# Two row halves of the array for the rows of an attention chunk, one sum of logits per routing group, one reciprocal for three chunks

## The chip, the cores and the metric

The kernel runs on one core of one Trainium2 chip. The metric is the device time of one execution in microseconds; a time given for a kernel is the median of several. One further execution is recorded by the hardware profiler, and all rows below are from that one.

## The reference

Sliding-window attention over 8 batches, 8 heads, 576 positions and 64 columns per head, and behind it a mixture of 8 experts in which each token goes to one expert:

```python
scores = scale * np.matmul(q, k.transpose(0, 1, 3, 2))
bias = slopes[:, None, None] * (-np.abs(rel).astype(np.float32))[None, :, :]
mask = (rel >= 0) & (rel < window)                      # window = 128
scores = np.where(mask, scores + bias[None], -1000000000.0)
attn = np.exp(scores - np.max(scores, axis=-1, keepdims=True))
attn = attn / (np.sum(attn, axis=-1, keepdims=True) + 1e-09)
x = attn @ v                                            # to 4608 tokens of 8 * 64 = 512
...
logits = x @ w_gate                                     # 512 x 8
expert_idx = np.argmax(logits, axis=1)
gate_w = softmax(logits)[np.arange(N), expert_idx]
out[mask] = gate_w[mask, None] * (np.maximum(x[mask] @ w1[e], 0.0) @ w2[e])   # for each expert e
```

Everything is float32.

## The kernel before

The 4608 queries are cut into 36 chunks of 128. A chunk takes four blocks of 32 queries, all of one batch, except for four chunks (the tails) that hold 64 queries of each of two batches. For a chunk, the steps are these; `g` is one of two groups of four heads:

- `scores` (L167, L176) writes bias and q.k into PSUM, each of the four 64x64 quadrants of TensorE's array for itself. `weigh` folds the window (L189), takes the maximum (L192) and lets ScalarE write the exponentials `pe` and, as a by-product, their sums `rsum` (L198).
- `guard` (L182) adds 1e-9 to the eight sums of a chunk on GpSimd.
- `transposes` (L211) turns `pe` with full 128x128 matmuls; ScalarE copies the result to `pT` (L213), GpSimd cuts the two key blocks out of it (L221, L223).
- `av` (L239) multiplies with v. The result is x transposed and not yet divided by the sums: for pair `p` of heads, 64 partitions hold one head and 64 the other. ScalarE copies it to `xT` (L286).
- `rows` (L244 to L257) turns it back to one row per token. The reciprocal of the chunk's sums is taken (L246). For each pair `p` of heads one matmul (L249) multiplies `xT[:, p, :]` with `iw_sb[:, p, :]`, which holds a 128x128 identity and beside it the 16 columns of the gate weights of both heads of the pair, so that the 144 columns of output are the row and each head's part of the logits. VectorE multiplies the logits' part and then the rows with the reciprocals (L254).
- `done` sums the parts of the logits over the eight heads (L1220) and stores the row to DRAM (`xd`) from the SP queue. A row has four pieces of 129 numbers, the last number of the last piece being kept for the gate.

After the last chunk of a routing group (`GROUPS`: 5, 5, 5, 6, 6, 3, 5 and 1 chunks), `route` works out each token's expert and place. Its matmuls use spare columns of the bank that `rows` wrote (`spare`).

The order of all this is written out by hand. A chunk `ch` begins at step `4 * ch`; the table `LAGS` says how many steps later each part is issued (`rows` 17 steps later), and `SPLIT` names the chunks whose second exponentials are issued three steps in, with the copy of an older chunk between them. Each engine works its own queue in order.

Behind attention, the experts' two layers (L711, L907) run from gathered rows with weights that were split into two parts; this and the tables of `route` are not touched.

Of the kernel before, what the change touches and what calls it, by code (L numbers as in the profile page):

```python
# [21 lines left out]
QB = 32  # L22
NP = H // 2
XW = 128 + 2 * E
SUB = 129
PITCH = 4 * SUB

# [7 lines left out]

def attention(ctx, tc, st, qT, kT, v, iw, load_c2, chunk_done, chunks, begun):
    nc = tc.nc
# [73 lines left out]
    make_bias()  # L111
    eps_sb = const.tile([128, H], F32, name="eps_sb")
    nc.gpsimd.memset(eps_sb, 1.0e-9)
# [66 lines left out]

    def guard(rsum):
        nc.gpsimd.tensor_tensor(out=rsum, in0=rsum, in1=eps_sb, op=ALU.add)  # L182

    def weigh(g, pe, rsum, s_ps, m, tail, lo, hi, later=False, add=True):
        s4 = s_ps.rearrange("p c n x -> p (c n) x")
        if m > 0:
            w = hi - 128
            sh = [128, 4, w]
            nc.vector.copy_predicated(out=s4[:, :, 0:w], mask=(tail_sb if tail else fold_sb)[:, 0:w].unsqueeze(1).to_broadcast(sh),  # L189
                                      data=s4[:, :, 128:128 + w])  # L190
        nmax = small.tile([128, 4], F32, name="nmax")
        nc.vector.tensor_reduce(out=nmax, in_=s4[:, :, lo:lo + 128], axis=AX.X, op=ALU.max, negate=True)  # L192

        def exps(pairs=range(2)):
            for n in pairs:
                for c in range(2):
                    h = 4 * g + 2 * n + c
                    nc.scalar.activation(  # L198
                        out=pe[:, h, :], in_=s_ps[:, c, n, lo:lo + 128], func=AF.Exp,
                        bias=nmax[:, 2 * c + n:2 * c + n + 1], scale=1.0, **(dict(accum_out=rsum[:, h:h + 1]) if add else {}),  # L200
                    )
            if add and g and 1 in pairs:
                guard(rsum)

        return exps if later else exps()
# [20 lines left out]
    def av(subs, pT, x_ps, pairs):  # L226
# [5 lines left out]
        for p, b, q, kb in whole:  # L232
# [4 lines left out]
            for c in range(2):  # L237
# [4 lines left out]
                )  # L242

    def rows(ch, subs, xT, rsum):  # L244
        rinv = small.tile([128, H], F32, name="rinv")
        nc.vector.reciprocal(out=rinv, in_=rsum)  # L246
        st["r_ps"] = r_ps = ps_r.tile([128, NP, 256], F32, name="r_ps")
        for p in range(NP):
            nc.tensor.matmul(out=r_ps[:, p, 0:XW], lhsT=xT[:, p, :], rhs=iw_sb[:, p, :], start=True, stop=True)  # L249
# [38 lines left out]
    def do(k, ch):  # L288
        if k == 9:
            return copy_x(ch)  # L290
        if k > 10:
            h = slice(4 * k - 44, 4 * k - 40)
            nc.vector.tensor_reduce(out=sums[ch][:, h], in_=pes[ch][:, h, :], axis=AX.X, op=ALU.add)
            return guard(sums[ch]) if k == 12 else None
        if k == 10:
# [5 lines left out]
        if k in (0, 4):  # L301
            if k == 0:
                pes[ch] = pp.tile([128, H, 128], F32, name="pe")
                sums[ch] = small.tile([128, H], F32, name="rsum", bufs=8)
            live[ch] = scores(subs, k // 4)
# [5 lines left out]
        elif k == 3:  # L311
            rows(ch, subs, xTs.pop(ch), sums.pop(ch))
        elif k == 6:
            transposes(subs, 1, pes[ch] if ch in SUMS else pes.pop(ch), pTs[ch])
        elif k == 7:
            xps[ch] = bank() if ch else ps_r.tile([128, NP, 256], F32, name="r_ps")[:, :, 0:128]
# [141 lines left out]
def spare(st, k, n):  # L458
    if st["step"] >= FREE_T:
        return st["bank"]()[:, k, 0:n]  # L460
    return st["r_ps"][:, k, XW:XW + n]

# [731 lines left out]
def attn_moe_kernel(ctx, tc, qT, kT, v, c2, iw, w12, out):  # L1194
# [9 lines left out]
    with ExitStack() as actx:  # L1204
        lgp = actx.enter_context(tc.tile_pool(name="lg", bufs=2))

        def begun(k):
            if k == 0:
                moe_setup(ctx, tc, st)
            else:  # L1210
                for j, n in enumerate(("tokh", "tokl")):
                    keep(tc, nc.vector.tensor_copy(out=st["hl"][:, :, j], in_=st[n]))

        def done(ch, subs, x_sb):
            c0, G = next((c, n) for c, n in GROUPS if c <= ch < c + n)
            g = ch - c0
            if g == 0:
                lgs["lg"] = lgp.tile([128, G, E], F32, name="lg")
            lg = lgs["lg"]
            nc.vector.tensor_reduce(out=lg[:, g, :], in_=x_sb[:, :, 128:XW].rearrange("q p (c e) -> q e p c", c=2),  # L1220
                                    axis=AX.XY, op=ALU.add)
            for lo in (0, 2):
                if lo == 2 and subs[0][0] == subs[2][0]:
# [3 lines left out]
                nc.sync.dma_start(out=st["xd"][t0:t0 + n].rearrange("t (p x) -> t p x", p=NP),  # L1227
                                  in_=x_sb[QB * lo:QB * lo + n, :, 0:SUB])
            if g == G - 1:
                groups = []  # L1230
# [16 lines left out]

        attention(actx, tc, st, qT, kT, v, iw, load_c2, done, chunks, begun)
    st["rc"] = ctx.enter_context(tc.tile_pool(name="rc", bufs=1))
# [6 lines left out]
def consts(moe_w_gate, moe_w1, moe_w2):  # L1256
# [4 lines left out]
    wg = moe_w_gate.reshape(NP, 128, E).transpose(1, 0, 2)  # L1261
    gate = np.zeros((128, NP, 2, E), wg.dtype)
    for c in range(2):
        gate[64 * c:64 * c + 64, :, c] = wg[64 * c:64 * c + 64]
    iw = np.concatenate([np.broadcast_to(np.eye(128, dtype=wg.dtype)[:, None], (128, NP, 128)), gate.reshape(128, NP, 2 * E)], axis=-1)
    parts = dict(ident=np.eye(128), seq=np.broadcast_to(np.arange(MAXOV), (128, MAXOV)), prof=np.broadcast_to(CAPS, (128, E)), rev=np.broadcast_to(np.arange(E, 0, -1), (128, E)), tokh=-64 * (back // 64), tokl=-(back % 64),
# [27 lines left out]
```

## Time and profile before

| | us |
|---|---|
| median of 3 runs (647.05 to 647.61) | 647.56 |
| profiled execution | 646.91 |
| its span, first to last instruction | 645.2 |
| TensorE busy in the span | 632.1 |
| VectorE busy | 390.9 |
| ScalarE busy | 314.1 |
| GpSimd busy | 299.2 |
| L249, 288 instructions, sum of their lengths | 41.4 |

In the rows, PE is a matmul on TensorE, PEld a load of its weights, which runs beside the matmuls. A form such as `64*128 128x72` is the rows and columns of the array that are used, and the output. One f32 matmul of the program shows as two loads and two matmuls. Lengths of matmuls overlap, since the array is a pipeline: the pace is read from the distance between starts. In grouped rows, "| a, b | c" is busy us in all, mean ns of one, and idle us of the engine just ahead, with what ended that.

### The profile page before, as it was taken

How to read it: one execution, taken by the hardware profiler on the slowest of the kernel's cores; microseconds unless marked ns; L12 is line 12 of the kernel's file. 1: busy time of each engine (PE TensorE's matmuls, PEld its weight loads, DVE VectorE, ACT ScalarE, POOL GpSimd, SP SyncE). 2: the span in 40 equal slices, each digit the busy share in tenths (PEclk: the TensorE clock that was granted, in tenths of full speed). 3: DMA queues.
4: the chain of work that ended last, by engine and by line, in shares of the span. 5: the costliest groups of instructions: out<-in, count | busy, mean ns of one | idle time of the engine just before them, and what ended most of it. 6: DMA issues, size and time to landing. Idle time of an engine off the chain costs nothing.

```text
span 645.2 us, 15063 instructions
## 1 busy us (share of the span) xinstructions
PE 632.1 (98%) x5681; PEld 540.2 (84%) x5681; DVE 390.9 (61%) x978; ACT 314.1 (49%) x947; POOL 299.2 (46%) x414
## 2 busy tenths in 40 slices
PE   8999999999998999999999999999999999999995
PEld 4888888888887988888988898898898888888884
DVE  6578888969898785545544654555455355346411
ACT  5878889888867324433333334334233333424311
POOL 5534657769446040166236707633660660561202
PEclk9999999999999999999999999999999999999999
DMA  9958998988734263372534325333442542534101
GB/s 312 301 153 216 220 260 237 217 258 240 193 69 103 54 196 98 130 273 75 186 128 151 108 78 183 113 94 139 142 122 83 165 122 87 185 107 143 65 0 62
DMA packets 57645, 97.90 MB, mean 152 GB/s; under 512 B 11669, under 2 KB 31765, under 8 KB 56674
## 3 DMA queue, kind: packets, MB, share of 16 engines
q1 hardware_dynamic: 49090, 76.89, 39.9%
q0 software_dynamic: 8336, 19.76, 10.6%
q8 instruction: 46, 0.75, 0.5%
q10 hardware_dynamic: 144, 0.26, 0.2%
q14 instruction: 29, 0.24, 0.1%
HBM read 77.91 MB, written 18.98 MB: 150 GB/s over the span
## 4 chain that ended last, share of the span: by engine, by line
PE 67%; ACT 0%; DVE 0%; issue 0%; POOLq 0%; POOL 0%; ACTq 0%
PE y_ps L907 32%; PE l_ps L711 30%; PE s_ps L711 2%; PE x_ps L672 1%; PE b_ps L239 1%; PE y_ps L867 1%; PE r_ps L249 0%; PE x_ps L867 0%; ACT pe L198 0%; POOLq L1060 0%; PE l_ps L683 0%; DVE y L915 0%; DVE nmax L192 0%; ACT e_xh L674 0%; DVE s_ps L189 0%
## 5 line engine op out<-in xcount | busy, mean ns | idle before, releaser
L714 ACT ACTIVATE hh<-l_ps 128x336 fp32r<-128x336 f32 (+7 forms) x104 | 45.9, 446 | 203.4 <-PE l_ps L711 176.9
L718 DVE SCALAR_TENSOR_TENSOR hl<-l_ps,hh 128x336 fp32r<-128x336 f32 (+7 forms) x104 | 51.7, 501 | 152.4 <-ACT hh L714 137.5
L691 POOL DMA_INDIRECT xg<-xd,od_idx x112 | 114.8, 1025 | 35.1 <-issue 34.8
L198 ACT ACTIVATE pe<-s_ps,nmax 128x128 f32<-128x128 f32 x288 | 102.9, 382 | 33.7 <-DVE nmax L192 27.0
L907 PE MATMUL y_ps<-wh,hh 128*128 128x512 f32 (+5 forms) x280 | 111.0, 397 | 0.0
L907 PE MATMUL y_ps<-wh,hl 128*128 128x512 f32 (+5 forms) x280 | 110.4, 394 | 0.0
L907 PE MATMUL y_ps<-wl,hh 128*128 128x512 f32 (+5 forms) x280 | 110.3, 394 | 0.0
L895 POOL DMA_INDIRECT out<-y,od_pidx x33 | 34.6, 1049 | 147.8 <-ACT y L913 141.2
L999 DVE TENSOR_TENSOR wl<-w_raw,wh 128x512 fp32r<-128x512 f32 x114 | 73.9, 690 | 32.0 <-ACT wh L995 27.4
L711 PE MATMUL l_ps<-xh,wh 128*128 128x304 f32 (+9 forms) x416 | 81.8, 318 | 0.3 <-DVE hl L718 0.3
L711 PE MATMUL l_ps<-xl,wh 128*128 128x304 f32 (+9 forms) x416 | 81.1, 316 | 0.3 <-issue 0.3
L711 PE MATMUL l_ps<-xh,wl 128*128 128x304 f32 (+9 forms) x416 | 81.0, 317 | 0.0
L711 PEld LDWEIGHTS l_ps<-xh,wh 128*128 128x128 f32 x416 | 68.0, 189 | 9.0 <-issue 1.2
L711 PEld LDWEIGHTS l_ps<-xl,wh 128*128 128x128 f32 x416 | 66.3, 189 | 2.3 <-issue 0.6
L711 PEld LDWEIGHTS l_ps<-xh,wl 128*128 128x128 f32 x416 | 66.4, 189 | 1.9
L239 PE MATMUL b_ps<-pT,v_sb 128*64 128x128 f32 (+2 forms) x1136 | 65.4, 265 | 0.4 <-ACT pT L213 0.4
L239 PEld LDWEIGHTS b_ps<-pT,v_sb 128*64 128x64 f32 (+1 forms) x1136 | 56.1, 136 | 10.0 <-issue 4.9
L907 PEld LDWEIGHTS y_ps<-wh,hl 128*128 128x128 f32 (+5 forms) x280 | 51.4, 184 | 13.7 <-DVE hl L718 0.2
L907 PEld LDWEIGHTS y_ps<-wl,hh 128*128 128x128 f32 (+5 forms) x280 | 51.5, 184 | 11.3
L907 PEld LDWEIGHTS y_ps<-wh,hh 128*128 128x128 f32 (+5 forms) x280 | 51.4, 184 | 10.4 <-ACT hh L714 0.5
L995 ACT CAST wh<-w_raw 128x1024 fp32r<-128x1024 f32 x57 | 59.5, 1044 | 1.0 <-DMA w_raw<-w 1.0
L198 ACT ACTIVATION_READ_ACCUMULATOR pe<-s_ps,nmax 128x1 f32 x272 | 59.6, 219 | 0.0
(225 smaller groups left out, 958.2 us busy)
## 6 DMA issues: line engine op xcount, KB each, us to landing
w_raw<-w SPq DMA_DIRECT2D x64, 512.0 KB
q_sb<-qT SPq DMA_DIRECT2D x39, 256.0 KB
xd<-x_sb SPq DMA_DIRECT2D x32, 258.0 KB
v_sb<-v SPq DMA_DIRECT2D x32, 256.0 KB
k_sb<-kT SPq DMA_DIRECT2D x7, 1152.0 KB
w_n<-w SPq DMA_DIRECT2D x4, 1024.0 KB
xg<-xd,od_idx POOLq DMA_INDIRECT x112
xd<-x_sb SPq DMA_DIRECT2D x8, 129.0 KB
```

The lines of the kernel that those rows point to most:

```text
L198: nc.scalar.activation(out=pe[:, h, :], in_=s_ps[:, c, n, lo:lo + 128], func=AF.Exp, bias=nmax[:, 2 * c + n:2 * c + n + 1], scale=1.0, **( ...
L239: nc.tensor.matmul(out=x_ps[64 * c:64 * c + 64, p, q], lhsT=blocks["v", b, m - 1 + kb][0:kk, D * h:D * h + D], rhs=pT[0:kk, kb, h, q], sta ...
L672: nc.tensor.transpose(out=x_ps[:, d, :], in_=g[:, SUB * d:SUB * d + 128], identity=st["ident"])
L691: ins = tc.nc.gpsimd.indirect_dma_start(out=g[:, s], out_offset=None, in_=parts, in_offset=bass.IndirectOffsetOnAxis(ap=idx[:, s], axis=0),)
L711: nc.tensor.matmul(out=ps, lhsT=a[:, 128 * d:128 * d + 128], rhs=b[:, d], start=(k == 0), stop=(k == 11))
L714: nc.scalar.activation(out=hh, in_=ps, func=AF.Relu)
L718: nc.vector.scalar_tensor_tensor(out=hl, in0=ps, scalar=0.0, in1=hh.bitcast(F32), op0=ALU.max, op1=ALU.subtract)
L867: nc.tensor.matmul(out=ps[m * g:m * g + n], lhsT=hrs[p][:, f, :], rhs=w2s[p][:, f % 4, w * g:w * g + w], start=f == 0, stop=f == 7)
L895: ins = nc.gpsimd.indirect_dma_start(**kw).ins
L907: nc.tensor.matmul(out=ys[t][0:n], lhsT=a[:, tl], rhs=b[:, 512:1024], start=(f == 0 and k == 0), stop=(f == 7 and k == 2))
L995: keep(tc, nc.scalar.copy(out=wh, in_=raw))
L999: keep(tc, eng.tensor_tensor(out=wl[:, sl], in0=raw[:, sl], in1=wh.bitcast(F32)[:, sl], op=ALU.subtract))
```

## The change

- `rows` uses two matmuls for each pair of heads, one in each half of the array's rows: head `c` of the pair takes partitions `64 * c` to `64 * c + 64` of `xT` as weights, and a constant of 72 columns (a 64x64 identity and the 8 columns of the gate weights) as what is streamed. The two write to two PSUM banks.
- The sums of three chunks lie in one tile. The addition of 1e-9 is done for all three on GpSimd, in the step in which the third chunk's last exponentials are issued (number 13 of the plan), and the reciprocal once, in `rows` of the first of the three.
- The products of logits and reciprocals go to a tile of the routing group, and one sum for the whole group replaces the sum for each chunk.
- The row is written to one of two fixed tiles whose pad column is zeroed once; it is stored without gaps.

```diff
+RW = D + E
...
-    iw_sb = const.tile([128, NP, XW], F32, name="iw_sb")
+    iw_sb = const.tile([128, NP, RW], F32, name="iw_sb")
...
+    rows_sb = [const.tile([128, NP, SUB], F32, name=f"x_sb{k}") for k in range(2)]
+    for x_sb in rows_sb:
+        nc.vector.memset(x_sb[:, :, 128:SUB], 0.0)
...
-    def guard(rsum):
-        nc.gpsimd.tensor_tensor(out=rsum, in0=rsum, in1=eps_sb, op=ALU.add)
...
     def rows(ch, subs, xT, rsum):
-        rinv = small.tile([128, H], F32, name="rinv")
-        nc.vector.reciprocal(out=rinv, in_=rsum)
-        st["r_ps"] = r_ps = ps_r.tile([128, NP, 256], F32, name="r_ps")
+        if ch % 3 == 0:
+            inv["of"] = small.tile([128, 3, H], F32, name="rinv", bufs=2)
+            nc.vector.reciprocal(out=inv["of"], in_=rsum)
+        rinv = inv["of"][:, ch % 3, :]
+        st["r_ps"] = r_ps = ps_r.tile([128, 2, 512], F32, name="r_ps")
+        r4 = r_ps[:, :, 0:NP * RW].rearrange("q c (p x) -> q p c x", p=NP)
         for p in range(NP):
-            nc.tensor.matmul(out=r_ps[:, p, 0:XW], lhsT=xT[:, p, :], rhs=iw_sb[:, p, :], start=True, stop=True)
-        x_sb = xp.tile([128, NP, XW], F32, name="x_sb")
-        for lo, n in ((128, E), (0, D)):
-            cols = slice(lo, lo + 2 * n)
-            split = lambda ap: ap[:, :, cols].rearrange("q p (c x) -> q p c x", c=2)
+            for c in range(2):
+                h = slice(64 * c, 64 * c + 64)
+                nc.tensor.matmul(out=r4[:, p, c, :], lhsT=xT[h, p, :], rhs=iw_sb[h, p, :], start=True, stop=True)
+        rows_sb.append(rows_sb.pop(0))
+        x_sb = rows_sb[-1]
+        for dst, at, n in ((logits(ch), D, E), (x_sb[:, :, 0:128].rearrange("q p (c x) -> q p c x", c=2), 0, D)):
             nc.vector.tensor_tensor(
-                out=split(x_sb), in0=split(r_ps),
+                out=dst, in0=r4[:, :, :, at:at + n],
                 in1=rinv.rearrange("q (p c) -> q p c", c=2).unsqueeze(3).to_broadcast([128, NP, 2, n]), op=ALU.mult)
         chunk_done(ch, subs, x_sb)
...
+        if ch % 3 == 2:
+            plan.setdefault(4 * ch + 3, []).append((13, ch))
...
+        if k == 13:
+            whole = sums["all", ch // 3]
+            return nc.gpsimd.tensor_tensor(out=whole, in0=whole, in1=eps_sb, op=ALU.add)
...
-            nc.vector.tensor_reduce(out=lg[:, g, :], in_=x_sb[:, :, 128:XW].rearrange("q p (c e) -> q e p c", c=2),
-                                    axis=AX.XY, op=ALU.add)
+            if ch == c0 + G - 1:
+                lg = lgp.tile([128, G, E], F32, name="lg")
+                nc.vector.tensor_reduce(out=lg, in_=lgs["all"].rearrange("q g p c e -> q g e (p c)"), axis=AX.X, op=ALU.add)
...
-                                  in_=x_sb[QB * lo:QB * lo + n, :, 0:SUB])
+                                  in_=x_sb[QB * lo:QB * lo + n])
```

How the rows of TensorE stand in the middle of attention, first in the kernel before. `s_ps` are the scores, `b_ps<-c_sb,pe` the transposes, `r_ps` the rows; `c_sb` holds the identity, and "x4" counts matmuls of the program:

```order
L176 MATMUL s_ps<-k_sb,q_sb 64x192 x8
L211 MATMUL b_ps<-c_sb,pe 128x128 x4
L249 MATMUL r_ps<-iw_sb,xT 128x144 x4
L211 MATMUL b_ps<-c_sb,pe 128x128 x4
L167 LDWEIGHTS eye_sb
```

The same place on TensorE in the changed kernel, whose line numbers are a little higher:

```order
L181 MATMUL s_ps<-k_sb,q_sb 64x192 x8
L211 MATMUL b_ps<-c_sb,pe 128x128 x4
L256 MATMUL r_ps<-iw_sb,xT 128x72 x8
L211 MATMUL b_ps<-c_sb,pe 128x128 x4
L172 LDWEIGHTS eye_sb
```

Nothing has moved; the four matmuls between the two blocks of transposes are eight of half the columns. This is so in all 36 chunks; 31 of these groups follow transposes of L211 and 33 are followed by them, and one follows scores.

VectorE's queue over one chunk, before; `nmax` is the maximum of the scores, `lg` the summed logits:

```order
L246 RECIPROCAL rinv<-rsum 128x8
L254 TENSOR_TENSOR x_sb<-r_ps,rinv 128x4x16
L254 TENSOR_TENSOR x_sb<-r_ps,rinv 128x4x128
L1220 TENSOR_REDUCE lg<-x_sb 128x8
L189 COPY_PREDICATED s_ps<-mask_sb,s_ps 128x4x128
L192 TENSOR_REDUCE nmax<-s_ps 128x4
```

And VectorE in the changed kernel over the last two chunks of the first routing group:

```order
L249 RECIPROCAL rinv<-rsum 128x24
L260 TENSOR_TENSOR lg_all<-r_ps,rinv 128x64
L260 TENSOR_TENSOR x_sb_134<-r_ps,rinv 128x4x128
L191 COPY_PREDICATED s_ps<-mask_sb,s_ps 128x4x128
L194 TENSOR_REDUCE nmax<-s_ps 128x4
L191 COPY_PREDICATED s_ps<-mask_sb,s_ps 128x4x128
L194 TENSOR_REDUCE nmax<-s_ps 128x4
L260 TENSOR_TENSOR lg_all<-r_ps,rinv 128x64
L260 TENSOR_TENSOR x_sb_133<-r_ps,rinv 128x4x128
L1237 TENSOR_REDUCE lg<-lg_all 128x40
```

The reciprocal stands in front of one chunk in three, and the sum of logits behind the last chunk of a group alone; what is left keeps its order.

More of the change, by code (lines that the diff above doesn't have):

```diff
@@ L33, in keep, with attention @@
     return ins if HELD[0] else tc.keep_in_program_order(ins)
-def attention(ctx, tc, st, qT, kT, v, iw, load_c2, chunk_done, chunks, begun):
+def attention(ctx, tc, st, qT, kT, v, iw, load_c2, logits, chunk_done, chunks, begun):
     nc = tc.nc
@@ L111, in attention @@
     make_bias()
-    eps_sb = const.tile([128, H], F32, name="eps_sb")
+    eps_sb = const.tile([128, 3, H], F32, name="eps_sb")
     nc.gpsimd.memset(eps_sb, 1.0e-9)
@@ L201, in exps @@
                     )
-            if add and g and 1 in pairs:
-                guard(rsum)
         return exps if later else exps()
@@ L242, in av @@
                 )
+    inv = {}
     def rows(ch, subs, xT, rsum):
[L245 to L253 removed]
+        if ch % 3 == 0:
[4 more added lines that the diff above has]
+        r4 = r_ps[:, :, 0:NP * RW].rearrange("q c (p x) -> q p c x", p=NP)
+        for p in range(NP):
+            for c in range(2):
[4 more added lines that the diff above has]
+        for dst, at, n in ((logits(ch), D, E), (x_sb[:, :, 0:128].rearrange("q p (c x) -> q p c x", c=2), 0, D)):
             nc.vector.tensor_tensor(
[L255 removed]
+                out=dst, in0=r4[:, :, :, at:at + n],
                 in1=rinv.rearrange("q (p c) -> q p c", c=2).unsqueeze(3).to_broadcast([128, NP, 2, n]), op=ALU.mult)
@@ L290, in do @@
             return copy_x(ch)
-        if k > 10:
+        if k in (11, 12):
             h = slice(4 * k - 44, 4 * k - 40)
             nc.vector.tensor_reduce(out=sums[ch][:, h], in_=pes[ch][:, h, :], axis=AX.X, op=ALU.add)
-            return guard(sums[ch]) if k == 12 else None
+            return
+        if k == 13:
+            whole = sums["all", ch // 3]
+            return nc.gpsimd.tensor_tensor(out=whole, in0=whole, in1=eps_sb, op=ALU.add)
         if k == 10:
@@ L303, in do @@
                 pes[ch] = pp.tile([128, H, 128], F32, name="pe")
-                sums[ch] = small.tile([128, H], F32, name="rsum", bufs=8)
+                if ch % 3 == 0:
+                    sums["all", ch // 3] = small.tile([128, 3, H], F32, name="rsum", bufs=3)
+                sums[ch] = sums["all", ch // 3][:, ch % 3, :]
             live[ch] = scores(subs, k // 4)
@@ L311, in do @@
         elif k == 3:
-            rows(ch, subs, xTs.pop(ch), sums.pop(ch))
+            rows(ch, subs, xTs.pop(ch), sums["all", ch // 3])
         elif k == 6:
@@ L315, in do @@
         elif k == 7:
-            xps[ch] = bank() if ch else ps_r.tile([128, NP, 256], F32, name="r_ps")[:, :, 0:128]
+            xps[ch] = bank() if ch else ps_r.tile([128, 2, 512], F32, name="r_ps").rearrange("p c (a x) -> p (c a) x", a=2)[:, :, 0:128]
             av(subs, pTs[ch], xps[ch], range(NP // 2))
@@ L460, in spare @@
         return st["bank"]()[:, k, 0:n]
-    return st["r_ps"][:, k, XW:XW + n]
+    return st["r_ps"][:, k // 2, NP * RW + 64 * (k % 2):NP * RW + 64 * (k % 2) + n]
 def route(tc, st, lg, c0, G, groups):
@@ L1212, in begun, with logits @@
                     keep(tc, nc.vector.tensor_copy(out=st["hl"][:, :, j], in_=st[n]))
+        def logits(ch):
+            c0, G = next((c, n) for c, n in GROUPS if c <= ch < c + n)
+            if ch == c0:
+                lgs["all"] = lgp.tile([128, G, NP, 2, E], F32, name="lg_all")
+            return lgs["all"][:, ch - c0]
         def done(ch, subs, x_sb):
             c0, G = next((c, n) for c, n in GROUPS if c <= ch < c + n)
[L1216 to L1220, printed above, removed]
-                                    axis=AX.XY, op=ALU.add)
+            if ch == c0 + G - 1:
+                lg = lgp.tile([128, G, E], F32, name="lg")
+                nc.vector.tensor_reduce(out=lg, in_=lgs["all"].rearrange("q g p c e -> q g e (p c)"), axis=AX.X, op=ALU.add)
             for lo in (0, 2):
@@ L1227, in done @@
                 nc.sync.dma_start(out=st["xd"][t0:t0 + n].rearrange("t (p x) -> t p x", p=NP),
-                                  in_=x_sb[QB * lo:QB * lo + n, :, 0:SUB])
-            if g == G - 1:
+                                  in_=x_sb[QB * lo:QB * lo + n])
+            if ch == c0 + G - 1:
                 groups = []
@@ L1246, in done @@
                     st["stages"].append([r, st["step"] + (c0 not in PACE), c0])
-        attention(actx, tc, st, qT, kT, v, iw, load_c2, done, chunks, begun)
+        attention(actx, tc, st, qT, kT, v, iw, load_c2, logits, done, chunks, begun)
     st["rc"] = ctx.enter_context(tc.tile_pool(name="rc", bufs=1))
@@ L1261, in consts @@
     wg = moe_w_gate.reshape(NP, 128, E).transpose(1, 0, 2)
[L1262 to L1265, printed above, removed]
+    eye = np.tile(np.eye(D, dtype=wg.dtype), (2, 1))
+    iw = np.concatenate([np.broadcast_to(eye[:, None], (128, NP, D)), wg], axis=-1)
     parts = dict(ident=np.eye(128), seq=np.broadcast_to(np.arange(MAXOV), (128, MAXOV)), prof=np.broadcast_to(CAPS, (128, E)), rev=np.broadcast_to(np.arange(E, 0, -1), (128, E)), tokh=-64 * (back // 64), tokl=-(back % 64),
```

## The prediction

> **What bounds the kernel now.** I read the busy times of the engines first, then the same by stretches, then the chain that ended last, and then TensorE's rows inside one chunk.
>
> ```profile
> span 645.2 us, 15063 instructions
> ...
> PE 632.1 (98%) x5681; PEld 540.2 (84%) x5681; DVE 390.9 (61%) x978; ACT 314.1 (49%) x947; POOL 299.2 (46%) x414
> ...
> PE 67%; ACT 0%; DVE 0%; issue 0%; POOLq 0%; POOL 0%; ACTq 0%
> ```
> ```profile
> 20.00:190.00 170.00, 169.75 (x2771) 141.51 (x2766) 137.52 (x355) 140.88 (x591) 104.94 (x173) 1.00 0.79 213
> 190.00:217.00 27.00, 25.23 (x324) 22.07 (x324) 21.99 (x70) 15.81 (x59) 10.94 (x17) 1.00 0.39 93
> 217.00:245.00 28.00, 28.00 (x197) 24.49 (x196) 22.87 (x110) 7.28 (x21) 8.01 (x8) 1.00 0.45 131
> 245.00:645.20 400.20, 392.76 (x2181) 341.87 (x2179) 194.65 (x418) 137.04 (x230) 163.20 (x181) 1.00 0.38 122
> ```
> In the stretches the columns are length, then busy time of PE, PEld, DVE, ACT and POOL, then the clock, the DMA share and GB/s. From 20 to 190 us, nearly all of attention, TensorE is without work for 0.25 us of 170; VectorE has 32 us to spare there, ScalarE 29, GpSimd 65. The chain that ended last is TensorE for 67% of the span and no other engine for 1%. The clock is full throughout. So a nanosecond more or less of TensorE's time in a chunk moves the end by as much, and time saved on the other engines counts only in the few places where TensorE waits.
>
> Busy is not the same as streaming, so the next view is TensorE in order of time (start, length, line, form, count):
>
> ```profile
> 121.55 0.36 PE L167 MATMUL s_ps<-bias_sb,eye_sb 64*64 64x384 bf16 x4
> 121.74 0.82 PE L176 MATMUL s_ps<-k_sb,q_sb 64*64 64x192 f32 x16
> 122.49 0.66 PE L211 MATMUL b_ps<-c_sb,pe 128*128 128x128 f32 x4
> 122.99 1.15 PE L249 MATMUL r_ps<-iw_sb,xT 128*128 128x144 f32 x8
> 123.97 0.60 PE L211 MATMUL b_ps<-c_sb,pe 128*128 128x128 f32 x4
> 124.50 0.36 PE L167 MATMUL s_ps<-bias_sb,eye_sb 64*64 64x384 bf16 x4
> ```
> ```profile
> 122.23 0.33 PE L176 MATMUL s_ps<-k_sb,q_sb 64*64 64x192 f32 x4
> 124.30 0.27 PE L211 MATMUL b_ps<-c_sb,pe 128*128 128x128 f32 x1
> ```
> Each f32 matmul of the program is two instructions here, so L249's four are x8. They start at 122.99 and the next block starts at 123.97: 0.98 us a chunk, 0.1225 us each.
>
> **The matmuls of the rows.** Removed: 8 instructions of 144 columns, 0.98 us. Added: 16 of 72 columns, in 8 pairs, one in the upper and one in the lower 64 rows of the array. If a pair runs side by side and streaming sets its pace, a pair takes half of 0.1225, 0.061 us. But each instruction has a weight load, still 128 columns wide:
>
> ```profile
> 232.44 0.97 PEld L683 LDWEIGHTS l_ps<-od_idx,sel 128*128 128x128 f32 x8
> L683 PEld LDWEIGHTS l_ps<-od_idx,sel x8: 190/192/193, 232.4 to 233.2; 128*128 128x128 f32 x8
> L683 PE MATMUL l_ps<-od_idx,sel x8: 203/284/284, 232.6 to 233.3; 128*128 128x42 f32 x8
> L176 PEld LDWEIGHTS s_ps<-k_sb,q_sb 64*64 64x64 f32 x1152 | 40.6, 134 | 3.1 <-issue 0.3
> L239 PEld LDWEIGHTS b_ps<-pT,v_sb 128*64 128x64 f32 x1008 | 51.8, 137 | 9.5 <-issue 4.9 <-POOL pT L221 3.5 <-POOL wl L1016 0.6
> 121.58 0.14 PEld L176 LDWEIGHTS s_ps<-k_sb,q_sb 64*64 64x64 f32 x4
> ```
> L683 is the nearest row: 128x128 f32 weights with only 42 columns to stream. Its eight loads start (0.97-0.19)/7 = 0.111 us apart, three times what 42 columns would need (42/144 of 0.1225 is 0.036): the load sets the pace. Halving the rows of the array does not shorten a load (134 ns at 64*64 against 137 at 128*64). Loads into different parts do run together: four of L176 are over in 0.14 us, as one alone. So I take 0.111 us a pair: 7 x 0.111 and the last pair's stream of 0.061 make 0.84 us, 0.14 less than now, 5.0 us over 36 chunks. The bounds: 0.061 a pair (stream sets it), 7 x 0.05 x 36 = 12.6 us less than this; 0.222 (the two loads follow each other), 7 x 0.111 x 36 = 28.0 us more. L683 has this width of load and this kind of data, so the middle value stands.
>
> The Trainium skill, TensorEngine Tiling (Array Packing), section Theoretical Speedup, promises up to 2x where one dimension is 64 or less. By it alone the rows would take half of 0.98 us, which is the third rival below; no row here shows a 64x128 form, and L683 speaks against it.
>
> **The changes of form.** Now L249 (128*128) stands between two blocks of L211 (128*128). Afterwards it is 64x128 between them, and the array changes form twice more a chunk. What such a change costs is in the rows above. Without one, L211's starts are (0.60-0.27)/3 = 0.11 us apart. From its last, at 124.30, to L167 (64*64) it is 0.20: 0.09 more. From L176's last four at 122.23 to L211 it is 0.26, where L176's own groups are (122.23-121.74)/3 = 0.16 apart: about 0.09 again. And the first weight load after a change lies open: L211's block of four lasts 0.66 behind L176 and 0.60 behind L249, so 0.06 more. For L249 itself one block follows L176:
>
> ```profile
> 22.04 0.33 PE L176 MATMUL s_ps<-k_sb,q_sb 64*64 64x192 f32 x4
> 22.31 0.51 PE L249 MATMUL r_ps<-iw_sb,xT 128*128 128x144 f32 x2
> ...
> L249 PE MATMUL r_ps<-iw_sb,xT x288: 285/286/391, 22.3 to 216.8; 128*128 128x144 f32 x144
> ```
> Its second start is at 22.31+0.51-0.29 = 22.53, 0.22 after the first instead of 0.12: 0.10 open. So entering costs 0.09+0.10 = 0.19 us in 35 chunks (the one of 22.31 pays today), 6.7 us; leaving costs 0.09+0.06 = 0.15 in 36, 5.4 us. Bounds: nothing, if 128x128 to 64x128 is no change of form to the array (no row has that pair), up to these 12.1 us. I take the full price, since 128*128, 128*64 and 64*64 all pay the same 0.09 among themselves.
>
> The Trainium skill, same page, Key Properties, says that changing the mode, though not the tile, drains TensorE; the pairs in this trace agree at 0.09 us, and by it the new pair pays too.
>
> **VectorE, GpSimd, the queues.**
>
> ```profile
> L192 DVE TENSOR_REDUCE nmax<-s_ps 128x4 f32<-128x512 f32 x72 | 49.6, 690 | 5.8 <-PE s_ps L176 3.5 <-PE r_ps L547 0.2 <-ACT pe L198 0.2
> L1220 DVE TENSOR_REDUCE lg<-x_sb 128x8 f32<-128x64 f32 x36 | 9.4, 260 | 0.0
> L246 DVE RECIPROCAL rinv<-rsum 128x8 f32<-128x8 f32 x36 | 6.9, 192 | 0.0
> L99 DVE TENSOR_SCALAR bias_sb<-back,slope 128x256 bf16<-128x256 f32 x4 | 1.6, 439 | 1.2 <-POOL back L88 1.2
> L182 POOL TENSOR_TENSOR rsum<-rsum,eps_sb x36: 194/200/395, 13.6 to 205.0; 128x8 f32<-128x8 f32 x36
> ```
> 24 of 36 reciprocals go: 24 x 0.19 = 4.6 us (the 12 left are a few ns longer). The 36 sums of logits (9.4 us) become 8; between the 64-element row (260 ns) and the 512-element row (690 ns) an element costs 0.96 ns, so 8 fixed parts of 0.2 and 2304 elements make 3.8 us, 5.6 less. GpSimd loses 24 of 36 additions, 4.8 us. Two memsets of the pad column are new ahead of L99, at most as long as the 64-element row, and lie in the 1.2 us for which VectorE waits there. The multiplications stay. All of this lies under TensorE's dense stretch, so I cost it at nothing there; the cover is TensorE's own queue. The group's addition on GpSimd waits for the third chunk's exponentials, and the selects on pT behind it wait for ScalarE's copy, which stands behind those exponentials anyway; the reciprocal comes six steps later, so this wait holds nobody. On the SP queue the constant iw is half as long and a chunk's row is stored as one piece of 2064 bytes instead of four of 516; no order of issues changes and the list of TensorE's waits names no transfer: nothing.
>
> VectorE's time counts where TensorE waits at the end of attention:
>
> ```profile
> 202.38 0.66 PE L211 MATMUL b_ps<-c_sb,pe 128*128 128x128 f32 x4 [0.78 <-ACT pT L213]
> ...
> 205.40 0.66 PE L211 MATMUL b_ps<-c_sb,pe 128*128 128x128 f32 x4 [0.51 <-ACT pT L213]
> 206.47 0.33 PE L239 MATMUL b_ps<-pT,v_sb 128*64 128x128 f32 x2 [0.41 <-ACT pT L213]
> ```
> These 1.7 us follow a stretch where VectorE is nearly full. Some 0.4 us a chunk saved there, and TensorE coming later itself, shorten them: between 0 and 1.7 us, I take 0.9; late next is ScalarE's copy itself, which the change leaves.
>
> **The sum.** -5.0 + 6.7 + 5.4 - 0.9 = +6.2 us. The profiled execution took 646.91 us (span 645.2 and 1.7 around it), 0.65 under the median of 647.56. So 653.1 for such an execution, 653.8 as a median.
>
> **The rivals.** (1) Slower still: the two weight loads of a pair follow each other. +28.0 us, 681.8. The 0.14 us of four L176 loads speaks against it. (2) Faster: the drains are paid but 64-row loads are quick enough that streams set the pace. 653.8 - 12.6 = 641.2. It decides from a pair time under 0.086 us, where 7 x 36 gaps give back the 6.2. L683 speaks against it; for it only that no 64x128 load is in the trace. (3) Faster by most: streams set the pace and no change of form is felt, so the rows take 0.49 us instead of 0.98: -17.6 - 0.9, 629.1. (4) Faster: loads set the pace, but 128x128 to 64x128 is no change of form: -5.0 - 0.9, 641.7. That all shown pairs of forms cost 0.09 speaks against it. (5) No change: the drains are paid, but the first loads hide in them, so 35 x 0.10 and 36 x 0.06, 5.7 us, go: 648.1. The block at 22.31 speaks against it. That the change does less than it says is no rival: the program holds the 64x128 forms in every chunk.
>
> Rival (3) is what the Trainium skill's factor of two in Theoretical Speedup would give.
>
> **How the numbers follow.** The forecast has 0.66, with its own range of 650.5 to 657 (pair time 0.01 us either way is 2.5 us, the waits 0 to 1.7). Rival (1) 0.06, (2) 0.10, (3) 0.04, (4) 0.08, (5) 0.06. Slower is 0.66+0.06 = 0.72, faster 0.22, the same 0.06; 0.2% or 1.3 us is about what a measurement can tell here. The range goes from 641 to 657: it takes in rivals (2), (4) and (5) and leaves out (1) and (3), 0.10, and some tail.
>
> **What would show it.** In the profile after, the rows' line has 576 matmuls of 64*128 and 72 columns; its weight-load starts come in twos 0.11 us apart (0.06 would be rival 2, 0.22 rival 1). The last L211 before it to its first start is 0.20 us, not 0.11, and its second pair is another 0.10 late; the L211 block behind it lasts 0.66, not 0.60. From the rows' first start to the next L211 is about 1.03 us instead of 0.98. VectorE's busy time falls by about 10 us and GpSimd's by 5 with no gain before 190 us. I am wrong if those gaps are missing, or if TensorE's stretch from 20 us holds idle time that I have not seen here.

## The result: 654.56 us, 7.0 us slower

The changed kernel takes 654.56 us (654.11 to 654.65), the kernel before 647.54 (647.05 to 647.61) on the same chip: a ratio of 1.0108, with a 95% interval of 1.0094 to 1.0123. The forecast was 653.8, inside a range of 641 to 657. The profiled execution took 654.11 us.

The page of the changed kernel, and its stretches of time (the columns are those of the prediction):

```profile
span 652.4 us, 15541 instructions
...
PE 640.5 (98%) x5969; PEld 539.8 (83%) x5969; DVE 388.5 (60%) x928; ACT 314.9 (48%) x947; POOL 295.0 (45%) x390
```
```profile
20.00:190.00 170.00, 170.00 (x2898) 135.65 (x2893) 129.99 (x299) 138.27 (x578) 99.00 (x148) 1.00 0.70 212
190.00:217.00 27.00, 26.48 (x414) 22.03 (x415) 23.90 (x64) 17.45 (x67) 12.46 (x19) 1.00 0.31 84
217.00:245.00 28.00, 27.88 (x235) 24.57 (x232) 22.53 (x111) 7.33 (x20) 8.01 (x8) 1.00 0.43 130
245.00:652.40 407.40, 398.30 (x2210) 346.10 (x2208) 197.69 (x426) 138.34 (x235) 163.37 (x181) 1.00 0.39 121
```

VectorE has 7.5 us less to do in the first stretch and GpSimd 5.9. TensorE is now without work for nothing of these 170 us, and it has only got later. The same chunk as in the prediction, in TensorE's order of time, then a closer view of the first two pairs, and then the weight loads and the rows' line as a whole:

```profile
125.60 0.66 PE L211 MATMUL b_ps<-c_sb,pe 128*128 128x128 f32 x4
126.19 1.11 PE L256 MATMUL r_ps<-iw_sb,xT 64*128 64x72 f32 x16
127.23 0.66 PE L211 MATMUL b_ps<-c_sb,pe 128*128 128x128 f32 x4
127.82 0.36 PE L172 MATMUL s_ps<-bias_sb,eye_sb 64*64 64x384 bf16 x4
```
```profile
125.99 0.27 PE L211 MATMUL b_ps<-c_sb,pe 128*128 128x128 f32 x1
126.19 0.33 PE L256 MATMUL r_ps<-iw_sb,xT 64*128 64x72 f32 x2
126.36 0.39 PE L256 MATMUL r_ps<-iw_sb,xT 64*128 64x72 f32 x4
```
```profile
126.19 0.97 PEld L256 LDWEIGHTS r_ps<-iw_sb,xT 64*128 64x128 f32 x16 [0.17 <-issue]
...
L256 PEld LDWEIGHTS r_ps<-iw_sb,xT x576: 182/188/188, 22.0 to 221.6; 64*128 64x128 f32 x192
L256 PE MATMUL r_ps<-iw_sb,xT x576: 272/272/327, 22.0 to 221.6; 64*128 64x72 f32 x192
```

Eight pairs of loads: 0.97 us less the length of one, 0.188, over seven distances is 0.112 us a pair. A pair does run side by side, but no faster than one 128-wide load. From L211's last start at 125.99 to the first pair is 0.20 us, where the matmuls of 144 columns followed after 0.11. From the first pair to the next L211 (126.19 to 127.23) is 1.04 us; it was 0.98. And the L211 block behind lasts 0.66 instead of 0.60. Half as many rows, half as many columns, and the chunk is 0.21 us longer: 0.09 + 0.06 + 0.06.

The prediction's block of this chunk stood at 122.49, so by here the kernel is 3.1 us late. Just ahead of the last chunks, at 188 us, the same instructions of TensorE are 5.65 us late: 29 blocks have cost about 0.21 each, and the start of this execution was 0.33 us quicker. Then the end of attention gives some back. TensorE's waits between 185 and 230 us, the kernel before in the first fence and the changed one in the second, and the changed kernel's partner of the row at 206.47:

```profile
PE b_ps L211 <- ACT pT L213: 1.3, 2, 0.8
PE b_ps L239 <- ACT pT L213: 0.4, 1, 0.4
PE r_ps L537 <- DVE x_sb L254: 0.3, 1, 0.3
```
```profile
PE b_ps L239 <- ACT pT L213: 0.4, 1, 0.4
```
```profile
210.85 1.97 PE L239 MATMUL b_ps<-pT,v_sb 128*64 128x128 f32 x32 [0.39 <-ACT pT L213]
```

The two waits of L211 (1.3 us) and the one of L537 (0.3) are gone, the one of L239 is still there, and the delay has come down to 210.85 - 206.47 = 4.4 us. Behind it stand three more blocks of the rows, between the routing and the first experts; over them the delay grows by 0.25, 0.16 and 0.32 us. Most of the rest is lost in the experts' layers, which the change does not touch. TensorE there, first before, then changed:

```profile
284.71 0.78 PE L711 MATMUL l_ps<-xh,wl 128*128 128x336 f32 x4
...
286.26 0.41 PE L711 MATMUL l_ps<-xl,wh 128*128 128x336 f32 x1 [0.31 <-issue]
286.51 0.40 PE L907 MATMUL y_ps<-wh,hh 128*128 128x512 f32 x1
```
```profile
289.86 0.78 PE L724 MATMUL l_ps<-xh,wl 128*128 128x336 f32 x4
291.41 0.56 PE L724 MATMUL l_ps<-xl,wh 128*128 128x336 f32 x2 [0.77 <-issue]
292.13 0.56 PE L724 MATMUL l_ps<-xl,wh 128*128 128x336 f32 x2 [0.17 <-issue]
292.53 0.39 PE L920 MATMUL y_ps<-wh,hh 128*128 128x512 f32 x1
```

At 284.71 the delay is 5.15 us, at 286.51 it is 6.02: in the middle of a group of matmuls TensorE stands idle for nothing that the profile shows ("issue"). A second such gap at 469 us adds 0.55. So of the span's 7.2 us more, 4.4 stand at the end of attention, 0.75 come while the last groups are routed (the three last blocks), 1.4 in those two gaps, and the rest, some 0.6, mostly behind TensorE's last matmul.

### The profile page after: what moved, and what is told of

Same layout as the page of the kernel before. It is cut to its first block, busy times and chain, and to the rows that moved or that the text cites. A ratio compares the mean times of both kernels' runs of the same rounds, so it can differ in the third digit from the quotient of the medians.

```text
span 652.4 us, 15541 instructions
## 1 busy us (share of the span) xinstructions
PE 640.5 (98%) x5969; PEld 539.8 (83%) x5969; DVE 388.5 (60%) x928; ACT 314.9 (48%) x947; POOL 295.0 (45%) x390
## 4 chain that ended last, share of the span: by engine, by line
PE 84%; issue 8%; DVE 3%; POOL 2%; ACT 1%; POOLq 0%; ACTq 0%; DVEq 0%
PE y_ps L920 26%; PE l_ps L724 26%; PE b_ps L239 9%; PE s_ps L181 6%; PE b_ps L211 6%; PE r_ps L256 5%; PE s_ps L172 3%; PE s_ps L724 1%; POOL out L908 1%; DVE nmax L194 1%; DVE s_ps L191 1%; POOL xg L704 1%; PE x_ps L685 1%; ACT pe L200 1%; PE y_ps L880 1%
## 5 line engine op out<-in xcount | busy, mean ns | idle before, releaser
L221 POOL TENSOR_SCALAR_AFFINE_SELECT pT<-pT 128x512 f32<-128x512 f32 x56 | 36.0, 643 | 67.2 <-ACT pT L213 67.1
L239 PE MATMUL b_ps<-pT,v_sb 128*64 128x128 f32 (+2 forms) x1136 | 65.3, 265 | 0.4 <-ACT pT L213 0.4
L239 PEld LDWEIGHTS b_ps<-pT,v_sb 128*64 128x64 f32 (+1 forms) x1136 | 56.2, 136 | 9.9 <-issue 4.6
```

Source lines behind the costliest of these rows:

```text
L239: nc.tensor.matmul(out=x_ps[64 * c:64 * c + 64, p, q], lhsT=blocks["v", b, m - 1 + kb][0:kk, D * h:D * h + D], rhs=pT[0:kk, kb, h, q], sta ...
```

## Experiments

The kernel before took 647.26 us beside the first four, 645.49 beside the next four, on another chip, and 647.15 beside the last four, again on the first chip. Ratios are against these; in the text "late" and "early" compare the starts of the same instructions of TensorE with the one profile of the kernel before, at the times of that profile.

### The row products alone

```diff
 # kernel before, with
+            for c in range(2):
+                h = slice(64 * c, 64 * c + 64)
+                nc.tensor.matmul(out=r4[:, p, c, :], lhsT=xT[h, p, :], rhs=iw_sb[h, p, :], start=True, stop=True)
 # reciprocal, guard, sum of logits and stores per chunk, as before
```

> The kernel before with the row products alone in two halves of the array (64x128, 72 columns); reciprocal, sum of logits and store stay one per chunk. Theory (TensorE pays for two changes of form a chunk and for weight loads): the rows of TensorE read as in the changed kernel, 0.217 us a chunk more, about +7.5 us; VectorE is not relieved, so the waits at the end of attention shrink only because TensorE comes later: 653.5 to 656 us. Rival (the slowdown comes from the other parts: later sums, fixed tiles, other stores): within 1 us of the kernel before, 647.5.

654.39 us (ratio 1.0119, 1.0103 to 1.0134). The products alone lose as much as the whole change. That the totals agree so closely is partly chance: up to 284 us of the kernel before's time this version is 6.3 us late and the changed kernel 5.15, and the changed kernel then loses more than the difference in the first gap shown above, which is missing here, while the one at 469 us is longer here. TensorE's order of time shows the same block:

```profile
126.30 1.11 PE L253 MATMUL r_ps<-iw_sb,xT 64*128 64x72 f32 x16
127.34 0.66 PE L212 MATMUL b_ps<-c_sb,pe 128*128 128x128 f32 x4
```

### Everything else alone

```diff
 # changed kernel, with
-                nc.tensor.matmul(out=r4[:, p, c, :], lhsT=xT[h, p, :], rhs=iw_sb[h, p, :], start=True, stop=True)
+            nc.tensor.matmul(out=r_ps[:, p, 0:XW], lhsT=xT[:, p, :], rhs=iw_sb[:, p, :], start=True, stop=True)
```

> The changed kernel with the row products put back to four 128x128 matmuls of 144 columns; group sums, one reciprocal for three chunks and the stores stay changed. Theory: nothing gained in the dense stretch, the waits of TensorE at its two ends shrink: 645.0 to 647.0 us. Rival (the other parts cost the time): 652 to 655. Second rival (they are worth nothing at all): 647.5.

648.76 us (1.0024, 1.0015 to 1.0033): a miss. Up to 188 us this kernel is 0.7 us late, at 213 us 0.6 early, since the waits of L211 are gone as expected. It then loses 0.8 us while the last groups are routed and 1.9 in the experts' layers, where TensorE stands idle for 1.6 us with nothing shown to wait for. The last section of the experiments takes this up.

### Eight products over the full height

```diff
 # changed kernel, with a constant of 8 x 72 columns in which the other head's 64 rows are zero
-                nc.tensor.matmul(out=r4[:, p, c, :], lhsT=xT[h, p, :], rhs=iw_sb[h, p, :], start=True, stop=True)
+                nc.tensor.matmul(out=r4[:, p, c, :], lhsT=xT[:, p, :], rhs=iw_sb[:, 2 * p + c, :], start=True, stop=True)
```

> The changed kernel, but each of the eight products of a chunk uses all 128 rows of the array, with zeros in the constant for the other head; 72 columns, no change of form, 16 weight loads one behind the other. Theory (a 128-wide load takes 0.111 us and sets the pace): 16 x 0.111 = 1.78 us a chunk instead of 0.98, +29 us less the 2 us of the other parts: 673 to 676 us. Rival (streaming sets the pace, 0.061 for 72 columns): 0.98 us a chunk as before, 645 to 647 us.

673.96 us (1.0413, 1.0394 to 1.0432). The distance is the load's, now without any change of form; order of time and the group of the loads:

```profile
136.28 1.90 PE L255 MATMUL r_ps<-iw_sb,xT 128*128 128x72 f32 x16
138.02 0.60 PE L211 MATMUL b_ps<-c_sb,pe 128*128 128x128 f32 x4
...
L255 PEld LDWEIGHTS r_ps<-iw_sb,xT 128*128 128x128 f32 x576 | 67.2, 192 | 0.3 <-issue 0.3
```

Sixteen instructions take 138.02 - 136.28 = 1.74 us, 0.109 each, for 72 columns, where 144 columns took 0.1225. The row halves do give their factor of two against this: a pair takes 0.112. But the kernel before had already half as many loads.

### Quadrants instead of halves

```diff
 # changed kernel, with
+            for a in range(2):
                 for c in range(2):
-                    nc.tensor.matmul(out=r4[:, p, c, :], lhsT=xT[h, p, :], rhs=iw_sb[h, p, :], start=True, stop=True)
+                    h, to = slice(64 * c, 64 * c + 64), slice(64 * a, 64 * a + 64)
+                    nc.tensor.matmul(out=r4[to, p, c, :], lhsT=xT[h, p, to], rhs=iw_sb[h, p, :], start=True, stop=True)
```

> The changed kernel with each product split once more, into the four 64x64 quadrants that the scores use: 16 products a chunk, weights 64 wide, 72 columns; still between the transposes, so two changes of form remain. Theory (load width sets the pace): a group of four takes 0.063 us instead of 0.111 for a pair, 0.37 us a chunk less than in the changed kernel: 640 to 643 us. Rival (the number of loads or instructions sets the pace, or the changes of form are all of the cost): 8 groups at 0.111 or more, 654 us or slower.

645.83 us (0.9979, 0.9969 to 0.9989): faster than the kernel before, though with less gain than expected. A load is now 64 wide, four run side by side, and in the trace a group of four follows the one before it by 0.0625 us, as expected. Order of time in a chunk and ahead of one, then TensorE's waits from 20 to 190 us:

```profile
122.03 0.73 PE L257 MATMUL r_ps<-iw_sb,xT 64*64 64x72 f32 x32
122.69 0.66 PE L211 MATMUL b_ps<-c_sb,pe 128*128 128x128 f32 x4
```
```profile
114.79 0.36 PE L172 MATMUL s_ps<-bias_sb,eye_sb 64*64 64x384 bf16 x4 [0.53 <-ACT pe L200]
...
PE s_ps L172 <- ACT pe L200: 1.1, 2, 0.5
```

The block is 0.66 us instead of 0.98 and pays the same two changes of form, about 0.17 us less a chunk with the open load behind it. The 29 blocks up to 188 us would be 4.9; 2.3 us stand there. Part of what is missing is waits where the kernel before has none: the scores wait 1.1 us for ScalarE's exponentials, and two other waits come to 0.5. At 213 us 3.5 stand; a wait for gathered rows and gaps in the experts' layers take 1.2 of them back by 300 us.

### Where the block stands: halves, and quadrants, behind the scores

```diff
 # changed kernel: the products get a step of their own, one earlier, behind a younger chunk's scores
+        if lags(ch)[3] == 17:
+            plan.setdefault(4 * ch + 16, []).append((14, ch))
...
+        if k == 14:
+            return row_products(ch, xTs.pop(ch))
```

> The changed kernel with its sixteen half-height row products (64x128) issued one step earlier on TensorE, directly behind the scores of a younger chunk (64x64), where they stood between two groups of 128x128 transposes; nothing else moves. My theory is that a change of the array's form costs about 0.09 us and that the first weight load behind it isn't hidden: between transposes the block pays two such changes a chunk, behind the scores it pays one more change than a chunk without row products (64x64 to 64x128, then to 128x128, where the scores paid one change of their own anyway). Worked out: 0.15 us a chunk less than the changed kernel over 33 chunks, so 649.0 to 651.0, about 649.5. Rival: the loss is the product's own length (weight loads that set the pace), wherever it stands: 654 to 655.

649.81 us (1.0073, 1.0060 to 1.0086). The absolute time lies in the range, but the kernel before was 2 us quicker on this chip: against it 4.3 us are lost, where 1.5 to 3.5 were expected and 7.0 are lost with the block between transposes. The order of time shows what a chunk pays now:

```profile
143.35 1.11 PE L252 MATMUL r_ps<-iw_sb,xT 64*128 64x72 f32 x16
144.39 1.09 PE L211 MATMUL b_ps<-c_sb,pe 128*128 128x128 f32 x8
145.42 0.36 PE L172 MATMUL s_ps<-bias_sb,eye_sb 64*64 64x384 bf16 x4
```

From the block to the scores behind the L211 group is 145.42 - 143.35 = 2.07 us. With the block between transposes it was 127.82 - 125.60 = 2.22, and before 124.50 - 122.49 = 2.01; the way in from the older scores is 0.25 us in all three. So the placement is worth the 0.15 us a chunk that were worked out, over two thirds of the 0.21 that a chunk lost, and the other 0.06 is what the block itself, to the next L211, is longer than before (1.04 against 0.98). What is missing is waits that the changed kernel has not: TensorE is without work for 1.9 us between 20 and 190 us, the scores for the exponentials, L239 for `pT`.

```profile
20.00:190.00 170.00, 168.07 (x2921) 138.31 (x2918) 134.12 (x302) 138.81 (x580) 99.69 (x150) 1.00 0.68 212
```

> The changed kernel with thirty-two quadrant products a chunk (64x64, in place of sixteen 64x128), issued one step earlier, directly behind the scores, which are 64x64 too, so that the block adds no change of form at all. Theory, by TensorE's terms alone: 0.45 us a chunk less than before, 15 us in all, 632; but in the quadrants between transposes TensorE began to wait for ScalarE's exponentials (1.1 us there), so a part is eaten: 632 to 642. Rival: another engine binds as soon as TensorE is shorter than before: 644 to 646.5, with waits of the scores for ScalarE or of the transposes for VectorE in the chunks.

642.50 us (0.9957, 0.9944 to 0.9970), 3.0 us faster than the kernel before and the fastest here, but a miss: it lies just above the 632 to 642 expected, and those were reckoned from 647.5. Against the kernel before, which was 2 us quicker on this chip, 5.5 to 15.5 us were to be gained. The gain is the rival's (1.0 to 3.5 us). No form changes for the block at all. A block in order of time, the stretch, and TensorE's waits in it:

```profile
58.50 0.67 PE L253 MATMUL r_ps<-iw_sb,xT 64*64 64x72 f32 x32
59.10 1.09 PE L211 MATMUL b_ps<-c_sb,pe 128*128 128x128 f32 x8
```
```profile
20.00:190.00 170.00, 163.59 (x3569) 137.02 (x3565) 141.12 (x323) 142.32 (x604) 102.73 (x154) 1.00 0.70 216
...
PE r_ps L253 <- issue: 1.4, 1, 1.4
PE b_ps L239 <- ACT pT L213: 1.3, 4, 0.3
...
PE s_ps L172 <- ACT pe L200: 0.6, 1, 0.6
```

0.60 us for what took 0.98. TensorE is 3.8 us early at 86 us and gains hardly more up to 188 (4.1): it has 6.4 us without work in the stretch now, though neither VectorE nor ScalarE is busy for more than 142 of 170. Of TensorE's waits in the stretch 2.6 us are for ScalarE, 1.4 for VectorE, and 1.4 are one gap without a shown cause. The chain that ended last runs over VectorE for a tenth of the span, where it was 0% before:

```profile
PE 68%; issue 11%; DVE 10%; ACT 4%; POOL 4%; DMA 1%; SPq 1%; POOLq 0%; DVEq 0%; ACTq 0%
```

> As the kernel with quadrants directly behind the scores, but with the sums, the reciprocal, the guard and the stores of the kernel before (logits summed per chunk, a reciprocal per chunk, rows stored out of 144-column tiles). The other parts of the change alone cost 1.2 us (0.7 to 1.6). Theory: that loss sits in the expert layers and comes back here: 0.5 to 2 us under the kernel with quadrants by the scores and the new sums. Rival: with TensorE shorter VectorE's work in the attention counts, and the old sums (7.5 us more of VectorE in 170) make it 1 to 5 us slower than that kernel.

644.93 us (0.9996, 0.9978 to 1.0015), in single runs from 642.05 to 648.92. With TensorE shorter the old sums cost 2.4 us against the kernel above, as the rival had it. The profile has one large wait, at the scores, again for nothing that it shows:

```profile
34.74 0.56 PE L177 MATMUL s_ps<-k_sb,q_sb 64*64 64x192 f32 x8 [2.60 <-issue]
```

So not all of the 2.4 us can be put down to VectorE's work.

### Sixteen matmuls more, to move TensorE's stream

```diff
 # kernel before, with
+        if s == 3:
+            w_ps = flat(bank())
+            for _ in range(16):
+                keep(tc, nc.tensor.matmul(out=w_ps[:, 0:16], lhsT=warm[:, 0:128], rhs=warm[:, 0:16], start=True, stop=True))
```

> The kernel before with sixteen small matmuls more (16 columns, their result unused) in an idle stretch of TensorE at about 6 us, so that every later instruction of TensorE stands elsewhere in its stream; nothing else is changed. Theory: the idle gaps inside the expert layers that wait for no engine come from how instructions are supplied, and their length depends on where the stream stands, so they change here though no work does: the gaps between 252 us and the end come to more than 0.6 us in sum (0.3 before), and the time is 647.8 to 649.5. Rival: they come from other edits (stores, sums), and stay at 0.3 us: 647.2 to 647.8.

645.80 us (1.0006, 0.9997 to 1.0014), no difference: the gaps did not come. But none of the four profiles on this chip has any from 252 us on, not even those of versions that share all the other parts with the changed kernel. So this run can't tell whether the place in the stream matters on a chip that shows gaps; it does show that they vary with the chip or the run.

### The other parts one by one

> The parts without the products once more (row products as four full-height matmuls; sums, reciprocal and stores as in the changed kernel), on whichever chip this comes to. They cost 1.5 us in the comparison of before, of which 2.1 us were gaps of TensorE inside the expert layers that wait for no engine, set against 0.7 us gained behind the last chunks. Theory: those gaps are the chip's and the moment's, not the change's; on another chip the difference to before is -1.0 to +0.7 us. Rival: the change brings them about by itself: +1.0 to +2.0 us again, in the same groups of the expert layers.

648.58 us (1.0022, 1.0012 to 1.0033), the rival's loss. The first time the gaps came to 1.6 us by this view, not to the 2.1 of the expectation, and stood in two groups, at 285 and 463 us. This run came to the same chip; the gaps at 285 us repeat, 1.0 us in all, and the one at 463 is missing, though the kernel is the same. TensorE's waits from 252 us on:

```profile
PE l_ps L721 <- issue: 1.0, 3, 0.5
```

```diff
 # kernel before: logits to a tile of the group, one reduce per group; the rows lie in two fixed tiles too
+    rows_sb = [const.tile([128, NP, XW], F32, name=f"x_sb{k}") for k in range(2)]
...
+            if ch == c0 + G - 1:
+                lg = lgp.tile([128, G, E], F32, name="lg")
+                nc.vector.tensor_reduce(out=lg, in_=lgs["all"].rearrange("q g p c e -> q g e (p c)"), axis=AX.X, op=ALU.add)
```

> The kernel before with one part of the change alone: logits of a routing group gathered in one tile and summed by one reduce, in place of one reduce per chunk (rows stored out of 144-column tiles, a reciprocal per chunk, products at full height, as before). Theory: VectorE isn't the bound in the attention, so its work saved is worth nothing but the wait at the group ends: -0.7 to +0.4 us against before. Rival: the sums at the ends of the groups come later and hold TensorE up: +1 us or more, with a wait of the routing matmuls for VectorE that before hasn't.

652.59 us (1.0097, 1.0079 to 1.0115), 5.4 us lost. The rival's number, but for the most part not by the rival's mechanism: behind the last sums the routing does wait for VectorE as it said, but that costs 0.5 us. VectorE in order of time, TensorE's wait for it, and two stretches of one microsecond (the clock is the third number from the end):

```profile
226.26 0.06 DVE L1169 MEMSET ov_cum<- 128x1 f32 x1 [2.81 <-DMA xd<-x_sb]
226.27 0.87 DVE L612 TENSOR_SCALAR l_lp<-c_sb,rank 128x128 bf16<-128x128 f32 x4
...
PE b_ps L620 <- DVE l_lp L612: 2.5, 1, 2.5
...
228.00:229.00 1.00, 1.00 (x8) 1.00 (x7) 1.00 (x5) 0.00 (x0) 0.46 (x1) 0.65 0.08 16
229.00:230.00 1.00, 1.00 (x6) 0.90 (x6) 0.89 (x3) 0.22 (x1) 0.74 (x1) 0.50 0.00 0
```

A memset of one column waits 2.8 us for the last store of the rows, and the tiles that the last routing needs are queued behind it. TensorE idles for 2.5 us. It takes up work at 226.6 us with the full clock, but from 228.3 to 231.7 us the granted clock is 0.50, so that the matmuls there are slower, by 0.2 us each for five of them, 1.6 us over the stretch: 4.1 us in all. That the memset's tile has come to lie on memory that the store reads would explain the wait; no view shows the addresses. The changed kernel has no such wait and the version without the products 0.3 us of it, so it is a trap of this version and not a price of the change. From 20 to 188 us the version neither gains nor loses more than 0.1 us: the sums saved are hidden there.

```diff
 # kernel before: rows in two tiles of 129 columns, logits in a tile of their own
-                                  in_=x_sb[QB * lo:QB * lo + n, :, 0:SUB])
+                                  in_=x_sb[QB * lo:QB * lo + n])
```

> The kernel before with one part alone: rows in two tiles of 129 columns, so that each store of a chunk reads one stretch per partition, logits in a tile of their own (sums, reciprocals, products as before). The stores make up the fall from 57645 to 43822 packets. Theory: the transfers are hidden and cost nothing either way: -0.4 to +0.4 us against before. Rival: the stores' other timing is what lengthens the gaps inside the expert layers: +1 to +2 us, and then the sums kernel shows its loss again on the same chip.

649.25 us (1.0027, 1.0016 to 1.0039), 2.1 us lost. The profiled execution was the slowest of the seven, at 650.15: it loses 0.95 us in the first 12 us, which need not be the version's, and then nothing up to 214; 0.5 us follow up to 245, and after that the gaps. TensorE's waits in the experts' layers and the longest of them:

```profile
PE l_ps L715 <- issue: 1.9, 4, 0.9
...
465.88 0.30 PE L715 MATMUL l_ps<-xh,wl 128*128 128x304 f32 x1 [0.89 <-issue]
```

This fits the rival, that the stores' timing lengthens the gaps. But the version with the logits alone has the same gaps at 285 us with the stores of before. Both have the two fixed tiles in place of the pool's. The version below has no such tiles and no gap at 285 us, though one of 0.4 us at 463. What the tiles have to do with it stays open.

```diff
 # kernel before: one guard and one reciprocal for three chunks
+        if ch % 3 == 0:
+            inv["of"] = small.tile([128, 3, H], F32, name="rinv", bufs=2)
+            nc.vector.reciprocal(out=inv["of"], in_=rsum)
```

> The kernel before with one part alone: one guard on GpSimd and one reciprocal on VectorE for three chunks, in place of one of each per chunk. Theory: both are hidden: -0.4 to +0.4 us against before. Rival: the guard of three chunks comes behind the third chunk's exponentials, so the first chunk's rows wait for it, and VectorE falls behind: +0.5 to +1.5 us, with a wait of the row products' buffers or of the routing for VectorE in the chunks.

646.43 us (0.9989, 0.9980 to 0.9998), 0.7 us faster, a little more than the 0.4 expected. TensorE's waits between 185 and 230 us are down to

```profile
PE b_ps L234 <- ACT pT L208: 0.4, 1, 0.4
```

so this part alone is enough to take away the 1.3 us of L211 at the end of attention, and no wait appears for the guard. It is not the only part that does: with the logits alone 0.3 us of the 1.3 are left, with the stores alone all of them.

The three parts do not add up: alone they make +5.4, +2.1 and -0.7 us, together +1.4.

## Why the prediction was right, point by point

- **The pair is paced by its load.** Taken 0.111 us, measured 0.112, and the version over the full height shows 0.109 a load with no other suspect. L683, a line of quite another part of the kernel, was the right row to read it from: same width, same kind of data, fewer columns. The number of instructions is not the cause: 32 quadrant instructions take 0.66 us where 16 in halves take 1.04. The factor of up to two that the Trainium skill gives in TensorEngine Tiling (Array Packing), Theoretical Speedup, is there against loads of the same width (0.109 us for one, 0.112 for a pair; 1.74 us to 1.04 for a block, with the entry's open part), and is not there against half as many matmuls with twice the columns (0.98 us).
- **128x128 to 64x128 is a change of form.** Taken 0.09 us each way, measured 0.20 against 0.11 at the entry. The Trainium skill, same page, Key Properties, says that a change of mode drains TensorE; these 0.09 us agree with it.
- **The first load behind it lies open.** At the entry 0.10 us was taken; the second pair stands 0.166 us behind the first, so 0.05. At the exit 0.06 was taken and measured; but the last pair takes about 0.05 more than the 0.061 I counted. That the two errors cancel is luck: 1.04 us from first pair to L211 against 1.03.
- **The rest hidden, but for the end of attention.** Taken -0.9 us, measured -1.6: the two waits of L211 that were named (1.3) and the one of L537 (0.3). The reciprocals alone and the logits alone each take most of the 1.3 away. What VectorE saves was over-read, without effect on the time, as it is hidden: about 10 us were forecast, and its two lines in the changed kernel give 16.3 - 8.9 = 7.4. A sum of a group takes 0.68 us where 0.48 was reckoned, and a reciprocal of 24 columns is 100 ns longer than one of 8, not a few.

```profile
L1237 DVE TENSOR_REDUCE lg<-lg_all 128x40 f32<-128x320 f32 (+3 forms) x8 | 5.4, 679 | 0.0
L249 DVE RECIPROCAL rinv<-rsum 128x24 f32<-128x24 f32 x12 | 3.5, 292 | 0.0
```

- **What the sum did not have.** Idle gaps in the experts' layers, 1.4 us beyond those of before, in which TensorE waits for nothing that the profile shows. By the terms of the sum alone the time would have come out near 652.7: at 284 us, behind all 36 blocks and ahead of the gaps, the delay is 5.15 us (about 7.1 for the blocks, as the sum had it, -1.6 for the waits, and -0.3 that the start was quicker). The gaps and half a microsecond behind the last matmul bring it to 654.6. The forecast of 653.8 lies between; the mechanism of the blocks was right, but that the number came within 0.8 us is in part luck. "I cost it at nothing" was right for the stretch under TensorE's cover and wrong for the whole program: the parts besides the products cost 1.4 us alone (measured twice), with the products nothing that can be told (654.56 against 654.39), and with the quadrants behind the scores they gain.

Rivals (1), (2) and (3) fall to the pair's 0.112 us and (4) to the 0.20. Rival (5) falls to the 0.166 and to L211's 0.66, though half of the open load at the entry is hidden, as it said of the whole.

## To carry to other kernels

Here a matmul with few columns is as long as its weight load (0.109 to 0.112 us for loads 128 wide, with 42 or 72 columns; 0.0625 for a group of four loads 64 wide), so cutting rows and columns in half helped only where the load's own width was cut too: 64x64 quadrants gained where 64x128 halves lost. Put products where the array already has their form, and price a block of another form at two changes and two open loads, here 0.15 us a chunk more than in a place where one change is paid anyway. Read that price before writing the code, from any line that has the same width of load and few columns.

## What the runs showed that I had not expected

- TensorE's gaps without a shown cause stand inside groups of the experts' layers at the same two places (some 285 and 463 us), from 0 to 2 us in all. The four profiles on the second chip have none, whatever the version. On the first chip the six experiments with the two fixed tiles for the rows, and the changed kernel, have 0.8 to 1.3 us of them at 285 us; the two experiments without such tiles have none there, and the kernel before 0.3. At 463 us they come and go even for one kernel (0.3 us and nothing in the two runs of the parts without products). Which of instruction supply, transfers and memory places brings them about is open.
- A wait of TensorE of 2.5 us was followed by a granted clock of 0.50 for 3.4 us, which began 1.7 us after the wait had ended and cost 1.6 us on top of it. A gap of 2.6 us in another version (with the old sums, at 32 us) was followed by nothing of the kind: the clock there stays at 1.00. So the length of a wait alone does not decide it.
- With the quadrants behind the scores, TensorE is idle for 6.4 of 170 us while no other engine is busy for more than 84% of it. That the latency of the chain from scores over VectorE and ScalarE to `pT` is then the limit is read from the chain and the waits; no run tested it.
